# Attention followed by a squared-relu feed-forward layer, float32, one core: fewer rows and fewer waits for the first values, and other times for four half sums

## The chip, the cores and the metric

The kernel runs on one core of one Trainium2 chip. The metric is the time of one execution on the device in microseconds; several executions are timed and their median is given. One further execution is taken by the hardware profiler, and all profile lines come from it.

A core has engines that run side by side, each with its own queue of instructions in a fixed order: PE (matrix products, with PEld for its weight loads), DVE, ACT and POOL (elementwise work), and SP, which here issues all transfers. The transfers are carried out by 16 DMA engines. An instruction waits at the head of its queue until its operands are there, and everything behind it waits with it.

## The reference

```
# q, k, v: (4, 8, 768, 64), w_in: (512, 2048), w_out: (2048, 512), all float32
k_sum = k.reshape(B, H, 24, 32, D).max(axis=3)      # block maxima of the keys
v_sum = v.reshape(B, H, 24, 32, D).mean(axis=3)     # block means of the values
scores_l = scale * q @ k^T, only where |i - j| < 16
scores_s = scale * q @ k_sum^T + log(32)
a = softmax over [scores_l, scores_s]
x = a @ [v, v_sum]                                  # (3072 tokens, 512)
out = relu(x @ w_in) ** 2 @ w_out
```

## The kernel before

**Attention.** The 4 x 768 queries are cut into 48 groups of 64. A group's local keys are 94 rows of its batch, to which 24 block maxima are added; its values are a tile of 128 partitions with 24 rows of block means and the local values. Groups 0 to 7 are worked singly: their values lie in lent tiles, block means in rows 0 to 23 and local values from row 24 on. Later groups are worked in pairs and share three fixed value tiles in turn (`kinds["v"]`): rows 0 to 7 zero, block means in rows 8 to 31, local values from row 32 on.

**The first groups' values.** For the first 11 groups the host lays out `vF`, 128 rows for each, zeros included, and `load_v` (L648) loads all 128 rows into the tile. The block means of batch 0 come from six loads of v, products with an averaging matrix on PE (L590) and a copy by DVE (L607, task VS0). Then each group's tile gets its 24 rows of means: by a transfer on SP (`load_s`, L659) or, for groups 0, 1, 6 and 7 (`COPIED`), by a copy on POOL (`copy_s`, L662). Because `load_v` writes all rows, both wait for it as well as for the means. The scores of a group are L694 (single groups) or L721 (pairs), the product with the values is L986, and its result is split into two float32r parts, xh (L1070) and xl (L1073).

**Feed-forward.** Weights are float64-wide words that are turned into pairs of float32r tiles (loads L1116, then L1119 to L1136). The 3072 tokens are six units of 512. Units 0 and 1 are worked plainly (L1183, L1207). Units 2 and 3, and 4 and 5, are worked with Strassen-like block products that need sums of weight blocks: for the second product in L1795, and for units 4 and 5 also for the first product (L1632, the block products). The sums of w_in for the latter are made by `combine_in(p)`, one for each of eight pairs p of weight tiles: for pairs 0 to 3 from the tiles that are still in place, for pairs 4 to 7 from tiles kept in DRAM and read back (tasks IL, L1358). IR (L1362, DVE) adds the two parts of a tile, IA (L1387, DVE) makes four sums, IH (L1394, ACT) and IW (L1397, DVE) split them, IS (L1400, SP) stores them to `scr_t`. The block products load them from there in chunks (L1619). All tiles of `combine_in` come from a ring of three buffers ("t") that other steps use too.

**The order of the work.** Each step is a task with an engine, an estimated cost, a key, tasks it comes after, and buffers it takes and uses. `Plan.order` simulates the engines with these estimates: a free engine takes the ready task with the lowest key whose `begin` time has come; a transfer counts its issue, its bytes at 350 GB/s behind the earlier ones, 1.9 us of latency and `late`, an extra that a task can state (`LATE` is 5.0). The order in which tasks start in this simulation is the order in which they are emitted on each engine's queue. So a changed cost, key or dependency can change the order of later work on every engine. `IN_AT` gives the nominal time of each pair's half sums, from which the keys of its tasks are made; nominal times are not the times of the profile. The tasks named in `FIRST` (the loads LV0 to LV7 of the first values among them) go first in a written order; all other transfers begin at 16 us of the simulation at the earliest.

Of the kernel before, what the change touches and what calls it, by code (L numbers as in the profile page):

```python
# [20 lines left out]
P = 128  # L21
BLOCK = 32
WINDOW = 16
TQ = 64
LOC = TQ + 2 * WINDOW - 2
NEG = -1.0e30
LINE = 256
SQ = 32
# [4 lines left out]
EARLY = 8  # L33
FIRST_S = 10
SINGLE = 3
NV = 3
# [3 lines left out]
LATE = 5.0  # L40
# [6 lines left out]
TURNED, DEEP_TURNS = 2, 8  # L47
SOON_KEY, LATE_KEY = 2.0, 14.0
ONE_PAIRS = 13, 15, 17, 19, 21
IN_AT = 228.0, 240.0, 252.0, 334.0, 346.0, 360.0, 424.0, 438.0  # L50
EARLY_SUM = 25.0
VISITS = (
    (4, 5, 0), (5, 6, 1), (None, 7, 0), (6, 8, 0), (7, 9, 0), (8, 10, 0), (9, 11, 0), (10, 12, 0), (None, 13, 0),
# [17 lines left out]
def first_key(w, S):  # L71
    return min(max(TQ * w - WINDOW + 1, 0), S - LOC)

# [52 lines left out]
class Plan:  # L126
# [13 lines left out]
    def add(self, name, engine, cost, emit, key, after=(), take=(), use=(), size=0, begin=0.0, behind=None, late=0.0):  # L140
        t = Task(name, engine, cost, emit, key, [a for a in after if a is not None], list(take), list(use), size, begin)
        t.behind, t.late = behind, late
        t.index = len(self.tasks)
        self.tasks.append(t)
        for b in t.take + t.use:
            b.users.append(t)
        return t
# [71 lines left out]
def attention_then_relu2_ffn(  # L219
# [9 lines left out]
    nc = tc.nc  # L229
    B, DMODEL, S = kT.shape  # L230
    D = qW.shape[1] // 2
    H = DMODEL // D
    NT, DM = out.shape
    NF = wW.shape[1]
    NPAIR = H // 2
    NB = S // BLOCK
    KEYS = NB + LOC
    HALF_W = SQ + 2 * WINDOW
# [18 lines left out]
    add = plan.add  # L257

    kinds = {}
# [95 lines left out]
    for i, (v, n, _) in enumerate(VISITS):  # L355
        k = 0
# [95 lines left out]
        nc.gpsimd.memset(ends[:, FRONT + NPAIR * (NB + S) :], 0.0)  # L452

    t_ends = add("ends", "POOL", 0.3, clear_ends, -85)

# [31 lines left out]

    def clear_a():  # L490
        nc.gpsimd.memset(kinds["a"].tiles[0][:SQ, : 2 * H * SQ], 0.0)

    def clear_turns():
        x = kinds["a"].tiles[0][:SQ, : 2 * H * SQ].rearrange("c (i e) -> c i e", i=2)
# [37 lines left out]
    vs_bufs = {}  # L532
# [105 lines left out]
    def loads_v(g):  # L638

        b, w = divmod(g, NW)  # L640
        due = wanted(g)
        vv = v_bufs[g]
        early = g < EARLY

        def load_v():
            if g < vF.shape[0]:

                nc.sync.dma_start(out=vv.tile, in_=vF[g])  # L648
                return

            k0 = TQ * w - WINDOW + 1
            r0, r1 = max(0, -k0), min(P - SQ, S - k0)
            cuts = (r0, SQ, P - SQ) if r0 else (0, P - SQ) if r1 == P - SQ else (0, 2 * SQ, r1)
            for r0, r1 in zip(cuts, cuts[1:]):
                nc.sync.dma_start(out=vv.tile[SQ + r0 : SQ + r1, :], in_=vS[b, k0 + r0 : k0 + r1, :])  # L655

        def load_s():
            r = 0 if early else PAD
            nc.sync.dma_start(out=vv.tile[r : r + NB, :], in_=vs_bufs[b].tile[:NB])  # L659

        def copy_s():
            nc.gpsimd.tensor_copy(out=vv.tile[:NB, :], in_=vs_bufs[b].tile[:NB])  # L662

        lv = t_LV[g] = [
            add(f"LV{g}", "SP", 0.45, load_v, due - 20, behind=t_QL[g] if early else t_LV[g - 1][0], take=[] if early else [vv],
                use=[vv] if early else [], size=4 * (P if g < vF.shape[0] else LOC) * DM, begin=due - 36)
        ]
        if not (g < EARLY or w < NV or (b == 0 and g < EARLY + NV)):
            return
        ts = t_VS[b]  # L670
        if g not in COPIED:
            key = FIRST_LS + g if early else due - 19
            lv.append(add(f"LS{g}", "SP", 0.45, load_s, key, ts + lv, use=[vv, vs_bufs[b]], size=4 * NB * DM))
        else:
            lv.append(add(f"LS{g}", "POOL", 0.62, copy_s, due - 8, ts + lv, use=[vv, vs_bufs[b]]))

    def mask_of(g):
        w = g % NW
# [313 lines left out]
    def visit(both, then=(), block_sums=None, due=None):  # L992
# [29 lines left out]
        for x in both:  # L1022
            if x not in t_LV:
                loads_v(x)
# [239 lines left out]
    t_WC, t_WI, t_RC, t_claim = {}, {}, [], []  # L1264
# [82 lines left out]
    def combine_in(p):  # L1347

        due = IN_AT[p]
        pair = [buf("t", 3, (P, 2 * DM), F32, f"ci{p}_{k}") for k in range(2)]  # L1350
        kept = 2 * p >= NQ
        raw = []
        for k in range(2):
            f = 2 * p + k
            x, ws = pair[k], w_parts[0, f]

            def load(f=f, x=x):
                nc.sync.dma_start(out=x.tile, in_=scr_i[f])  # L1358

            def whole(x=x, ws=ws):  # L1360
                a, b = (x.tile[:, :DM], x.tile[:, DM:]) if kept else (w.tile.bitcast(F32) for w in ws)
                nc.vector.tensor_tensor(out=x.tile[:, :DM], in0=a, in1=b, op=ALU.add)  # L1362

            t = None
            behind = raw[0] if k else t_claim[-1]
            if kept:
                t = add(f"IL{p}_{k}", "SP", 0.45, load, due - 8 + 0.1 * k, [t_WI[f]], take=[x], size=8 * P * DM, begin=due - 14, behind=behind)
                t_claim.append(t)
                raw.append(t)
            t = add(  # L1370
                f"IR{p}_{k}", "DVE", 0.6, whole, due + 0.1 * k, [t, *t_W[0, f]], take=[] if kept else [x],
                use=[x] if kept else ws, behind=None if kept else behind, begin=due - 6,
            )
            if not kept:
                t_claim.append(t)
                raw.append(t)
            t_IN[p, k] = t

        def of(i, k):
            return pair[i].tile[:, k * HALF : (k + 1) * HALF]  # L1380

        def add_up():
            for to, a, b, op in (
                (of(1, 2), of(1, 0), of(1, 1), ALU.add), (of(0, 2), of(1, 2), of(0, 0), ALU.subtract),
                (of(0, 3), of(0, 0), of(1, 0), ALU.subtract), (of(1, 3), of(0, 1), of(0, 2), ALU.subtract),
            ):
                nc.vector.tensor_tensor(out=to, in0=a, in1=b, op=op)  # L1387

        t2 = add(f"IA{p}", "DVE", 1.25, add_up, due + 1, [t_IN[p, 0], t_IN[p, 1]], use=pair)
        ts = []  # L1390
        for k in range(2):

            def high(x=pair[k]):
                nc.scalar.copy(out=x.tile[:, :DM].bitcast(F32R), in_=x.tile[:, DM:])  # L1394

            def low(x=pair[k]):
                nc.vector.tensor_tensor(out=x.tile[:, DM:].bitcast(F32R), in0=x.tile[:, DM:], in1=x.tile[:, :DM], op=ALU.subtract)  # L1397

            def store(k=k, x=pair[k]):
                nc.sync.dma_start(  # L1400
                    out=scr_t[p][2 * k : 2 * k + 2].rearrange("c p w x -> p w c x"),
                    in_=x.tile.rearrange("p (w c x) -> p w c x", w=2, c=2),
                )

            t3 = add(f"IH{p}_{k}", "ACT", 0.52, high, due + 2 + 0.1 * k, [t2], use=[pair[k]])
            t4 = add(f"IW{p}_{k}", "DVE", 0.6, low, due + 3 + 0.1 * k, [t3], use=[pair[k]])
            ts.append(add(f"IS{p}_{k}", "SP", 0.45, store, due + 4 + 0.1 * k, [t4], use=[pair[k]], size=8 * P * DM))
        t_IN[p] = ts
# [582 lines left out]
```

## Time and profile before

| | |
|---|---|
| runs | 594.16, 594.57, 597.3 us, median 594.57 us |
| profiled execution | 594.56 us |
| its span, first to last instruction | 592.8 us |
| instructions | 12694 |
| PE busy | 575.0 us, 97% of the span |
| DVE, ACT, POOL busy | 411.2, 354.8, 61.5 us |
| moved by DMA | 158.63 MB, 268 GB/s |
| mean granted PE clock | 0.997 |

How to read the lines: a timeline line has start and length in us, the engine, the line of the program, the operation, what it writes and reads, the shape and the number of instructions put together; in brackets the idle time of the engine before it and what released it. SPq is SP's queue; a DMA line there is the issue of a transfer, not its course. A line of waits has the engine and line that waited, the one it waited for, and us in total, number of waits and the longest. Where a wait is for several things, the profile names the one that came last by its records, which can be another than the true one. A line of a window has its bounds and length, then busy us and number of instructions of PE, PEld, DVE, ACT and POOL, the granted PE clock, the share of time that the DMA engines were busy, and GB/s.

### The profile page before, as it was taken

The page shows a single profiled execution, that of the slowest core. Times are in us where ns is not written, and L with a number is a line of the kernel's source. Part 1 is how long each engine was busy: PE and PEld are TensorE (multiplying, and loading weights), DVE is VectorE, ACT ScalarE, POOL GpSimd, SP SyncE. Part 2 cuts the span into 40 slices and gives each one's busy share as a digit, 9 for nine tenths or more (in the row PEclk, how much of TensorE's full clock was granted, in tenths as well). Part 3 has the DMA queues.
Part 4 walks back from the last instruction along what each step waited for, and adds up shares of the span by engine and source line. Part 5 has one row for each costly group of instructions (what it writes and reads, how often), then busy time and mean ns, then how long its engine had stood idle before and what let it go on. Part 6 is the DMA issues. An engine that isn't in the chain of part 4 may idle for free.

```text
span 592.8 us, 12694 instructions
## 1 busy us (share of the span) xinstructions
PE 575.0 (97%) x4724; PEld 469.0 (79%) x4724; DVE 411.2 (69%) x652; ACT 354.8 (60%) x801; POOL 61.5 (10%) x101
## 2 busy tenths in 40 slices
PE   7879999999999999999999998999998999999996
PEld 6677888888888788888788887878887888788885
DVE  5879997864466482387775798999936523897653
ACT  1879876965454545475652665655546757755542
POOL 4400001032634720000000000000000000000000
PEclk9989999999999999999999999999999999999999
DMA  8998994779999769578998789998799865567772
GB/s 310 324 350 270 328 310 160 234 210 369 329 355 318 260 202 326 190 250 274 329 310 239 245 288 329 351 345 265 233 342 338 275 194 159 150 195 228 197 224 99
DMA packets 98667, 158.63 MB, mean 268 GB/s; under 512 B 9791, under 2 KB 54591, under 8 KB 98606
## 3 DMA queue, kind: packets, MB, share of 16 engines
q1 hardware_dynamic: 98606, 157.82, 82.0%
q8 instruction: 38, 0.62, 0.4%
q14 instruction: 23, 0.19, 0.1%
HBM read 112.16 MB, written 45.88 MB: 267 GB/s over the span
## 4 chain that ended last, share of the span: by engine, by line
PE 85%; DMA 6%; DVE 4%; ACT 2%; SPq 1%; issue 1%; DVEq 0%
PE o L1795 25%; PE o L1207 15%; PE h L1183 14%; PE h L1481 10%; PE o L1632 10%; PE att L721 3%; PE x L986 3%; DMA ci<-scr_i 2%; DMA kb<-kT 2%; PE vps L590 1%; DMA w<-scr_s 1%; DVE kb L521 1%; PE att L986 1%; PE o L694 1%; SPq L655 1%
## 5 line engine op out<-in xcount | busy, mean ns | idle before, releaser
L1795 PE MATMUL o<-gh,w 128*128 128x512 f32 x448 | 120.9, 391 | 0.6 <-DMA w<-scr_s 0.6
L1779 ACT CAST gh<-g 128x512 fp32r<-128x512 f32 x112 | 69.0, 621 | 55.3 <-PE o L1795 34.0
L1795 PEld LDWEIGHTS o<-gh,w 128*128 128x128 f32 x448 | 83.5, 188 | 18.7 <-issue 1.1
L1784 DVE TENSOR_TENSOR gl<-g,gh 128x512 fp32r<-128x512 f32 x112 | 75.3, 685 | 20.1 <-ACT gh L1779 19.9
L1183 PE MATMUL h<-xh,w 128*128 128x512 f32 x240 | 74.8, 393 | 0.0
L1481 PE MATMUL h<-xh,w 128*128 128x512 f32 x224 | 69.9, 394 | 1.7 <-ACT r L1491 1.7
L1795 PE MATMUL o<-gl,w 128*128 128x512 f32 x224 | 69.2, 390 | 0.0
L1207 PE MATMUL o<-w,gh 128*128 128x512 f32 x240 | 61.8, 393 | 0.0
L908 ACT ACTIVATE p<-p,nm 128x88 f32<-128x88 f32 x120 | 42.7, 357 | 18.1 <-DVE nm L902 18.1
L1183 PEld LDWEIGHTS h<-xh,w 128*128 128x128 f32 x240 | 44.6, 188 | 10.0 <-DVE w L1136 0.2
L1207 PEld LDWEIGHTS o<-w,gh 128*128 128x128 f32 x240 | 44.5, 188 | 9.9 <-DVE w L1136 0.3
L1481 PEld LDWEIGHTS h<-xh,w 128*128 128x128 f32 x224 | 41.6, 188 | 10.9 <-ACT r L1491 1.9
L1795 PEld LDWEIGHTS o<-gl,w 128*128 128x128 f32 x224 | 42.0, 188 | 9.0 <-DVE gl L1784 0.2
L1183 PE MATMUL h<-xl,w 128*128 128x512 f32 x120 | 46.7, 389 | 0.0
L1491 ACT ACTIVATE r<-h 128x512 f32<-128x512 f32 x32 | 19.1, 596 | 41.1 <-PE h L1481 41.1
L1481 PE MATMUL h<-xl,w 128*128 128x512 f32 x112 | 43.6, 389 | 0.0
L1632 PE MATMUL o<-w,w 128*128 128x512 f32 x140 | 34.8, 391 | 0.0
L1207 PE MATMUL o<-w,gl 128*128 128x512 f32 x120 | 33.5, 389 | 0.0
L1197 DVE TENSOR_TENSOR gl<-r,gh 128x512 fp32r<-128x512 f32 x30 | 23.5, 787 | 14.2 <-ACT gh L1194 9.3
L1772 DVE TENSOR_TENSOR g<-g 128x512 f32<-128x512 f32 x48 | 32.2, 685 | 0.8
L1274 POOL TENSOR_TENSOR cr<-w 128x512 f32<-128x512 f32 x16 | 23.3, 1475 | 80.0 <-DVE w L1136 72.2
L1632 PEld LDWEIGHTS o<-w,w 128*128 128x128 f32 x140 | 26.1, 188 | 6.3 <-DVE u L1664 0.5
(195 smaller groups left out, 982.4 us busy)
## 6 DMA issues: line engine op xcount, KB each, us to landing
raw<-wW SPq DMA_DIRECT2D x32, 512.0 KB
w<-scr_s SPq DMA_DIRECT2D x64, 256.0 KB
w<-scr_a SPq DMA_DIRECT2D x48, 256.0 KB
w<-scr_i SPq DMA_DIRECT2D x38, 256.0 KB
scr_t<-ci SPq DMA_DIRECT2D x16, 512.0 KB
turn<-ta SPq DMA_DIRECT2D x80, 96.0 KB
a<-turn SPq DMA_DIRECT2D x20, 384.0 KB
w<-scr_t SPq DMA_DIRECT2D x28, 256.0 KB
```

Source lines behind the costliest of these rows:

```text
L908: nc.scalar.activation(x, x, AF.Exp, bias=nm.tile[:, n : n + 1], accum_out=nm.tile[:, H + n : H + n + 1])
L986: nc.tensor.matmul(x_of(i)[h % 2 * D : (h % 2 + 1) * D, h // 2, :], lhsT=v_bufs[g].tile[:rows, h * D : (h + 1) * D], rhs=av[:rows, 2 * c : ...
L1183: nc.tensor.matmul(cut(h), lhsT=lhs.tile[:, k * P : (k + 1) * P], rhs=rhs[:, k, c0 : c0 + n], start=(i == 0), stop=(i == 3 * KT - 1),)
L1197: lambda: nc.vector.tensor_tensor(out=cut(gl), in0=cut(r), in1=cut(gh).bitcast(F32), op=ALU.subtract),
L1207: nc.tensor.matmul(o_of(o, t), lhsT=terms[i][0].tile[:, (t - t0) * P : (t - t0 + 1) * P], rhs=terms[i][1].tile, start=(first and i == 0), ...
L1274: nc.gpsimd.tensor_tensor(out=raw.tile[:, k * DM : (k + 1) * DM], in0=ws[k][0].tile.bitcast(F32), in1=ws[k][1].tile.bitcast(F32), op=ALU.add)
L1481: nc.tensor.matmul(h.tile, lhsT=lhs.tile[:, k * P : (k + 1) * P], rhs=rhs[:, k, c0 : c0 + TU], start=(i == 0), stop=(i == 3 * KT - 1),)
L1632: nc.tensor.matmul(o.tile[:, bank], lhsT=chunk.tile[:, w * HALF + d * P : w * HALF + (d + 1) * P], rhs=xs[y][d], start=starts and i == 0, ...
L1772: lambda x=x, ins=ins, op=op: nc.vector.tensor_tensor(out=x.tile, in0=ins[0].tile, in1=ins[1].tile, op=op),
L1779: f"GH{s}_{n}", "ACT", 0.54, lambda x=x, gh=gh: nc.scalar.copy(out=gh.tile, in_=x.tile), due - 4, ready,
L1784: lambda x=x, gh=gh, gl=gl: nc.vector.tensor_tensor(out=gl.tile, in0=x.tile, in1=gh.tile.bitcast(F32), op=ALU.subtract),
L1795: nc.tensor.matmul(o.tile[:, d], lhsT=chunk.tile[:, w * HALF + d * P : w * HALF + (d + 1) * P], rhs=y.tile, start=begins and w == 0 and y ...
```

## The change

Three things change.

1. `vF` holds 96 rows (`FULL`) for each of the first 11 groups instead of 128, and `load_v` writes only these rows (from row 24 on for groups 0 to 7, from row 32 on for groups 8 to 10). The zero rows that the later groups need come from a new task "pads" on POOL, which clears 32 rows of the three fixed value tiles once. The tasks that put block means into a tile wait for the means (and the pads), not for the tile's values. For groups from 8 on the transfer of means is kept behind the issue of the values' load; the POOL copies of groups 6 and 7 get a `begin` of 20.5. The estimated bytes of every value load become those of 96 rows.
2. The nominal times of the half sums of w_in change: pairs 3, 4 and 5 from 334, 346 and 360 to 330, 344 and 358, pairs 6 and 7 from 424 and 438 to 444 and 456.
3. The loads of pairs 4 to 7 get a key 16 us ahead of the nominal time instead of 8, a `begin` 20 us ahead instead of 14, and count as landing 5 us later.

```diff
+FULL = 96
...
-IN_AT = 228.0, 240.0, 252.0, 334.0, 346.0, 360.0, 424.0, 438.0
+IN_AT = 228.0, 240.0, 252.0, 330.0, 344.0, 358.0, 444.0, 456.0
...
+    t_pads = []
...
+    def clear_pads():
+        for x in kinds["v"].tiles:
+            nc.gpsimd.memset(x[:SQ], 0.0)
+
+    t_pads.append(add("pads", "POOL", 0.8, clear_pads, -70))
...
-                nc.sync.dma_start(out=vv.tile, in_=vF[g])
+                r = NB if early else SQ
+                nc.sync.dma_start(out=vv.tile[r : r + FULL], in_=vF[g])
...
-                use=[vv] if early else [], size=4 * (P if g < vF.shape[0] else LOC) * DM, begin=due - 36)
+                use=[vv] if early else [], size=4 * FULL * DM, begin=due - 36)
...
-            lv.append(add(f"LS{g}", "SP", 0.45, load_s, key, ts + lv, use=[vv, vs_bufs[b]], size=4 * NB * DM))
+            lv.append(add(
+                f"LS{g}", "SP", 0.45, load_s, key, ts + t_pads, use=[vv, vs_bufs[b]], size=4 * NB * DM,
+                behind=None if early else lv[0],
+            ))
         else:
-            lv.append(add(f"LS{g}", "POOL", 0.62, copy_s, due - 8, ts + lv, use=[vv, vs_bufs[b]]))
+            lv.append(add(
+                f"LS{g}", "POOL", 0.62, copy_s, due - 8, ts, use=[vv, vs_bufs[b]], begin=20.5 if g > 1 else 0.0
+            ))
...
-                t = add(f"IL{p}_{k}", "SP", 0.45, load, due - 8 + 0.1 * k, [t_WI[f]], take=[x], size=8 * P * DM, begin=due - 14, behind=behind)
+                t = add(f"IL{p}_{k}", "SP", 0.45, load, due - 16 + 0.1 * k, [t_WI[f]], take=[x], size=8 * P * DM, begin=due - 20, behind=behind, late=LATE)
...
-    vF = np.zeros((EARLY + NV, P, H * D), v.dtype)
+    vF = np.zeros((EARLY + NV, FULL, H * D), v.dtype)
```

More of the change, by code (lines that the diff above doesn't have):

```diff
@@ L1962 @@
             k0 = first_key(g, S)
-            vF[g, S // BLOCK : S // BLOCK + LOC] = vS[0, k0 : k0 + LOC]
+            vF[g, :LOC] = vS[0, k0 : k0 + LOC]
         else:
             k0 = TQ * g - WINDOW + 1
-            vF[g, SQ:] = vS[0, k0 : k0 + P - SQ]
+            vF[g] = vS[0, k0 : k0 + FULL]
     w_in, w_out = inputs["moe_w_in"], inputs["moe_w_out"]
```

## The prediction

> **What bounds the kernel now.** I read the page first, then the waits of PE, then the busy time by stages, and last the order of time around each wait that the change can touch.
>
> ```profile
> PE 575.0 (97%) x4724; PEld 469.0 (79%) x4724; DVE 411.2 (69%) x652; ACT 354.8 (60%) x801; POOL 61.5 (10%) x101
> PE att L986 <- ACT t L1119: 2.6, 1, 2.6
> PE h L1481 <- ACT r L1491: 1.7, 1, 1.7
> PE o L1632 <- DVE v L1664: 1.7, 1, 1.7
> PE att L986 <- DVE nm L784: 1.5, 1, 1.5
> ```
>
> PE is busy for 575.0 of 592.8 us and the change takes no matmul away, so all that it can win lies in PE's 17.8 us of idle time. The waits show where: four single waits of 2.6, 1.7, 1.7 and 1.5 us. The stages say when:
>
> ```profile
> 10.00:20.00 10.00, 9.36 (x188) 6.08 (x188) 8.26 (x23) 5.67 (x27) 4.22 (x13) 1.00 1.04 365
> 20.00:30.00 10.00, 7.99 (x224) 6.71 (x224) 8.48 (x27) 8.39 (x37) 2.76 (x4) 1.00 0.97 318
> 30.00:40.00 10.00, 6.51 (x96) 5.90 (x85) 6.97 (x15) 7.36 (x21) 0.00 (x0) 0.83 1.00 388
> 40.00:60.00 20.00, 20.00 (x107) 16.89 (x105) 19.30 (x31) 19.54 (x47) 0.00 (x0) 1.00 0.86 268
> 360.00:380.00 20.00, 18.25 (x108) 14.72 (x107) 17.98 (x33) 13.44 (x35) 0.00 (x0) 1.00 1.02 330
> 380.00:400.00 20.00, 19.40 (x138) 15.47 (x137) 19.02 (x33) 11.10 (x18) 0.00 (x0) 1.00 1.05 357
> 440.00:460.00 20.00, 18.30 (x81) 14.82 (x80) 11.35 (x20) 13.00 (x24) 0.00 (x0) 1.00 0.98 350
> ```
>
> The columns are PE, PEld, DVE, ACT, POOL, the granted clock, the DMA share and GB/s. From 10 to 40 us the DMA engines are full (1.04, 0.97, 1.00) and PE idles 6.1 of 30 us; from 40 us on PE has no idle at all, so what the start wins moves everything behind it. The other two waits stand at 360 to 380 and 440 to 460 us, again with full DMA engines. The change works on all three places.
>
> **Part 1, the first groups' values.** The eight early loads (L648) and three later ones shrink from 128 to 96 rows of 2 KB, the block means (L659, L662) no longer wait for them.
>
> ```profile
> qvpa_lent<-vF SPq DMA_DIRECT2D x8, 256.0 KB
> 16.24 0.81 DVE L607 COPY fv_lent<-vps 24x256 f32<-24x256 f32 x2
> 18.01 1.74 SPq L659 DMA_DIRECT2D qvpa_lent<-fv_lent  x2
> 22.53 2.15 SPq L659 DMA_DIRECT2D qvpa_lent<-fv_lent  x2
> 25.52 0.81 SPq L1116 DMA_DIRECT2D raw<-wW  x2
> SPq L1116 <- DMA qvpa_lent<-fv_lent: 0.3, 1, 0.3
> 23.75 0.38 PE L694 MATMUL o<-first 64*64 64x118 f32 x8
> 23.93 0.41 DVE L1073 TENSOR_TENSOR xl<-att,xh 128x256 fp32r<-128x256 f32 x1
> 25.64 1.23 PE L986 MATMUL att<-qvpa_lent 118*64 118x64 f32 x32 [1.51 <-DVE nm L784]
> ```
>
> The wait of 1.5 us is the value product of group 2 at 25.64. The profile names DVE, but the weight load that SP issues at 25.52 had itself waited for a copy of block means, the transfer issued eight before it (SP takes its eight semaphores in turn, so a transfer waits for the eighth before it to land). That copy, issued at 18.01, so landed at about 25.5, after 7.5 us in the queue, and it is this that PE waited for. The means were ready at 17.05 (16.24 + 0.81) and SP took them up at 18.01, so the old wait for the values cost nothing here; the time went in the queue behind earlier loads. Ahead of that copy stand eight value loads, each 64 KB smaller now: 0.524 MB, at 365 GB/s 1.44 us, at 318 GB/s 1.65 us. PE was free at 24.13 and the previous group's low half, which the same instruction counts on DVE, ended at 24.34. So the gain lies between 0 (the landing hangs on something else) and 1.51; I take 25.64 - 24.34 = 1.30.
>
> Moved with it: the two copies issued at 22.53 (2.15 us of SP) can now be issued with the first two, ahead of one q load and two weight loads. That pushes these three by up to 2.15 us on SP, less what the smaller loads give back. I take nothing: their users come behind the PE wait treated next. If that cover is gone, up to 2.15 - 1.44 = 0.7 us comes back.
>
> ```profile
> 6.40 0.52 POOL L491 MEMSET a<- 32x512 f32 x1
> 22.56 0.60 POOL L662 COPY qvpa_lent<-fv_lent 24x512 f32<-24x512 f32 x1 [0.68 <-DMA qvpa_lent<-vF]
> ```
>
> The three new clears have the shape of the row at 6.40: 3 x 0.52 = 1.56 us on POOL right behind it, where POOL then waits for PE's first scores. Uncovered they would hold back the first softmax by at most that; I take 0. The two copies from 22.56 on lose up to 0.68 us of waiting each on POOL, which no one on PE waits for: 0.
>
> The next wait, 2.6 us, is the one I leave:
>
> ```profile
> 32.71 1.78 PE L986 MATMUL att<-qvpa_lent 118*64 118x64 f32 x32 [2.55 <-ACT t L1119]
> q8 instruction: 1, 0.02, 1.9%
> 29.58:32.99 3.41, 0.86 (x49) 0.62 (x37) 3.31 (x11) 2.76 (x11) 0.00 (x0) 1.00 0.90 333
> 32.99:36.41 3.42, 3.42 (x40) 3.30 (x36) 1.18 (x3) 1.79 (x5) 0.00 (x0) 0.50 1.04 420
> ```
>
> The copies of means for groups 4 and 5 were issued from 22.53 on and, at 7.5 us like the first, had landed by 31; ACT's L1119 has no part in this product. The row of queue q8 is that of the stretch 29 to 33 us: one piece of PE's instruction stream comes in there, through the same full DMA engines. I read the 2.55 us as PE waiting for its instructions: it starts when PE has used up what it holds, and moves with PE. It keeps its length, so the 1.30 us pass through it. Behind it the clock is granted at half for 3.42 us; that costs up to 1.71 us of PE and I leave it too.
>
> **Part 2, half sums of pairs 3 to 5** (nominal 334, 346, 360 to 330, 344, 358; for the pairs read back from DRAM the load is planned 16 instead of 8 us ahead and counted as landing 5 us later).
>
> ```profile
> 355.48 0.40 SPq L1358 DMA_DIRECT2D ci<-scr_i  x1
> 361.82 0.69 DVE L1362 TENSOR_TENSOR ci<-ci 128x512 f32<-128x512 f32 x1 [1.82 <-DMA ci<-scr_i]
> 366.91 0.88 DVE L902 TENSOR_REDUCE nm<-p 128x8 f32<-128x704 f32 x1
> 368.89 0.57 ACT L1491 ACTIVATE r<-h 128x512 f32<-128x512 f32 x1
> 369.52 0.74 PE L1481 MATMUL h<-xh,w 128*128 128x512 f32 x2 [1.75 <-ACT r L1491]
> ```
>
> DVE stands still for 1.82 us in front of pair 4's second sum, whose load was issued at 355.48 and took 6.3 us. All behind it on DVE is late by that: the row maximum at 366.91, then the exponentials on ACT, then the relu queued behind them at 368.89, which frees the bank that PE wants: 1.75 us. The planner counted 0.45 + 1.50 + 1.90 = 3.85 us for this load (the program's constants); with 5 more it counts 8.85, over the 6.3 measured, so the sum moves behind its landing in DVE's order. Gain 1.75 at most. At the other end a sum that waits as now (1.82) in 380 to 400, where DVE has 0.98 us free, costs 0.84. I take 1.75: the one wait has one cause and the edit is larger than it.
>
> **Part 3, pairs 6 and 7** (424, 438 to 444, 456, loads as in part 2).
>
> ```profile
> 435.70 0.88 SPq L1358 DMA_DIRECT2D ci<-scr_i  x1
> 440.94 0.69 DVE L1362 TENSOR_TENSOR ci<-ci 128x512 f32<-128x512 f32 x1 [1.45 <-DMA ci<-scr_i]
> 444.22 0.69 DVE L1362 TENSOR_TENSOR ci<-ci 128x512 f32<-128x512 f32 x1 [2.59 <-DMA ci<-scr_i]
> 447.80 0.68 DVE L1664 TENSOR_TENSOR v<-o,v 128x512 f32<-128x512 f32 x1
> 464.88 0.71 SPq L1400 DMA_DIRECT2D scr_t<-ci  x1
> 483.19 4.40 SPq L1619 DMA_DIRECT2D w<-scr_t  x4
> ```
>
> The same picture: DVE waits 1.45 and 2.59 us for loads (435.70 to 444.22 is 8.5 us), and the sum at 447.80, which frees PE's bank, is late by enough to cost PE 1.70 us. Counted as 8.85 us and sought 20 us later, these sums no longer stand in front of their loads. DVE is busy 11.35 of 20 us here, so the work itself finds room. What is late next: the last store, issued at 464.88, comes up to 18 us later, 482.9, and the loads that first need it are issued from 483.19 on, ahead of PE's use. Bounds: 1.70 gained, or 0 when the loads are issued later too and DVE meets them as now. I take 1.70.
>
> **The sum.** 1.30 + 1.75 + 1.70 = 4.75 us. The profiled execution took 594.56 us (span 592.8 and 1.76 around it), the median of the runs is 594.57: 594.56 - 4.75 = 589.8 us.
>
> **Rivals.** (a) The start gives nothing: the freed queue is filled by weight loads of 512 KB, which keep eight in flight, and PE's next instructions come as late as before, so the second wait swallows the first's gain. For it: a larger load ahead costs 0.524 MB/333 GB/s = 1.57 us, as much as the gain. Against it: the stream of instructions is also asked for earlier. Time: 594.56 - 3.45 = 591.1.
>
> (b) More goes than I take: the shifted idle time no longer falls into one stretch of the clock, and the half-rate stretch after it is gone: 589.8 - 1.71 = 588.1. For it: PE was busy 0.86 of 3.41 us ahead of the half rate, and 1.30 us earlier it would be 2.2. Against it: where the stretches begin may differ between executions. [...] And if the 2.55 us are not the instruction stream but a landing behind the values, they go too: 589.8 - 2.55 - 1.71 = 585.5. [...]
>
> (c) One of the two DVE waits stays or turns up elsewhere, since every order after the start is worked out anew: 594.56 - 1.30 - 1.70 = 591.6, with a new wait of 1 us 592.6.
>
> (d) Slower: the last batch's keys.
>
> ```profile
> 282.70 3.52 SPq L958 DMA_DIRECT2D turn<-ta  x4
> 289.35 0.90 PE L721 MATMUL att<-kb,q 64*32 64x128 f32 x44 [0.52 <-DVE kb L521]
> ```
>
> PE already waits 0.52 us at 289.35 for keys, so their loads have no slack; the planner sets them by costs that change. Put behind the turned store that now follows them (282.70, 3.52 us) and the two loads of 512 KB that go with such a step (3.1 us at 333 GB/s), PE would wait 6.6 us more: 594.56 - 4.75 + 6.6 = 596.4. From a slip of 4.75 us it decides. Against it: nothing in the edit names these loads.
>
> **How the numbers follow.** Forecast 0.42, (a) 0.16, (b) 0.11, (c) 0.19, (d) or another wait of its size 0.12. About 0.5%, 3.0 us, is what a measurement of this kernel can tell from no change. Faster by more than that: the forecast, (b), and most of (a), whose 591.1 is just beyond: 0.62. Within: (c) and the rest of (a): 0.25. Slower: the upper part of (d) and of (c): 0.13. The range leaves out (d), the worst of (c), and 585.5: 587.8 to 594.0; for the forecast alone 588.8 to 590.8.
>
> **What would show it.** Right: PE's value product of groups 2 and 3 starts within 0.3 us of PE being free, near 24.3; the wait of about 2.5 us with a q8 row in it still follows, near 29 to 31; no DVE wait for ci<-scr_i above 0.5 us; PE's waits on L1491 and L1664 gone; the last scr_t store before 483. Wrong: a value product that still waits over 1 us near 25.5, new PE waits in 40 to 280 us, where there are none now, a DVE wait for ci<-scr_i again, or a wait for keys near 289 that has grown.

## The result, and the profile after

The change made the kernel slower: 598.58 us (median of 20 runs, 594.60 to 603.29) against 594.37 us for the kernel before in the same session (20 runs, 591.30 to 597.97). The ratio is 1.0068, with a 95% interval of 1.0045 to 1.0090. The ratios in this document are worked out from the single runs and leave out the few slow executions (at most one of a kernel, two of before beside it), so they are not quotients of the medians. The profiled execution of after took 598.27 us, its span 596.5. The forecast was 589.8 us, faster. Lines of the program that are named here stand 9 to 14 lower in after: L648 is now L657, L659 L668, L1119 L1133, L986 L1000, L1358 L1372, L1664 L1678, L1795 L1809; in the kernels with a written order further down they are another 33 lines lower, and in rows96_only up to 3 lower than in before.

The page's busy times:

```profile
PE 576.2 (97%) x4724; PEld 468.9 (79%) x4724; DVE 409.3 (69%) x652; ACT 354.9 (59%) x801; POOL 63.2 (11%) x104
```

The waits of PE (what waited and for what; us in all, times, the longest):

```profile
PE x L1000 <- DMA a<-turn: 2.3, 1, 2.3
PE att L1000 <- DMA raw<-wW: 2.1, 1, 2.1
PE x L1000 <- DMA w<-scr_s: 1.5, 1, 1.5
PE o L1809 <- DMA w<-scr_s: 1.5, 2, 0.9
PE t L863 <- DVE qvpa_lent L852: 1.3, 1, 1.3
PE o L1646 <- DVE u L1678: 0.9, 1, 0.9
```

The wait for ACT's relu (1.7) is gone, as forecast, that of the value product of group 2 (1.5) has given way to one of 0.8 for ACT, and the one near 450 us has fallen from 1.7 to 0.9. New ones stand in their place: transposes at the start that wait for DVE, and attention products in the second half that wait for transfers. By stages (PE, PEld, DVE, ACT, POOL, granted clock, DMA share, GB/s):

```profile
10.00:20.00 10.00, 9.36 (x188) 6.08 (x188) 8.26 (x23) 5.74 (x26) 4.42 (x14) 1.00 1.06 297
20.00:30.00 10.00, 7.13 (x148) 6.21 (x152) 7.08 (x21) 7.49 (x34) 1.76 (x4) 0.83 0.93 281
30.00:40.00 10.00, 7.10 (x167) 6.20 (x160) 7.38 (x20) 6.96 (x20) 0.00 (x0) 1.00 1.02 366
360.00:380.00 20.00, 19.89 (x114) 15.81 (x112) 18.47 (x34) 14.42 (x38) 0.00 (x0) 1.00 1.02 320
380.00:400.00 20.00, 17.02 (x127) 13.65 (x127) 16.70 (x30) 9.70 (x17) 0.00 (x0) 1.00 1.03 331
400.00:420.00 20.00, 17.73 (x132) 14.37 (x131) 17.70 (x29) 10.83 (x18) 0.00 (x0) 1.00 0.91 264
440.00:460.00 20.00, 19.08 (x84) 15.33 (x83) 10.37 (x18) 13.55 (x24) 0.00 (x0) 1.00 0.90 321
```

Two rows are to be read against those of before. From 10 to 20 us the DMA engines are as full as they were (1.06 against 1.04), but move 297 instead of 365 GB/s: the fewer bytes take the same time. This row parts all the profiles below in the same way: 295 to 322 GB/s in the ten kernels that load 96 rows, 353 to 395 in the eight that load 128. From 380 to 420 us PE is idle for 5.25 us where it was idle for 0.6, with DMA engines at 1.03 and 0.91, while 360 to 380 has gained 1.64. The row of before from 400 to 420 us:

```profile
400.00:420.00 20.00, 20.00 (x142) 16.26 (x142) 19.63 (x33) 11.87 (x20) 0.00 (x0) 1.00 0.87 261
```

The start of after in its timeline:

```profile
19.32 3.27 SPq L668 DMA_DIRECT2D qvpa_lent<-fv_lent  x4
22.73 0.43 DVE L1136 TENSOR_SCALAR raw<-raw 128x512 uint32<-128x512 uint32 x1 [2.01 <-DMA raw<-wW]
22.73 0.69 ACT L1133 ACTIVATE t<-raw 128x512 f32<-128x512 f32 x1 [2.51 <-DMA raw<-wW]
23.07 0.65 DVE L852 TENSOR_TENSOR qvpa_lent<-qvpa_lent,nm 128x472 f32<-128x472 f32 x1
23.48 1.24 SPq L1130 DMA_DIRECT2D raw<-wW  x2
23.86 0.63 PE L863 MATMUL t<-first,qvpa_lent 128*128 128x128 f32 x4 [1.30 <-DVE qvpa_lent L852]
26.77 1.98 PE L1000 MATMUL att<-qvpa_lent 118*64 118x64 f32 x32 [0.85 <-ACT qvpa_lent L833]
34.57 1.15 PE L1000 MATMUL att<-qvpa_lent 118*64 118x64 f32 x32 [2.13 <-DMA raw<-wW]
```

DVE and ACT stand still for 2.0 and 2.5 us in front of the first weight tile. Behind it on DVE is the multiplication that ends a group's softmax (L852), and PE's transposes wait 1.30 us for that. The four copies of block means now stand in one row at 19.32, and the second weight load follows at 23.48. In the timeline of before the same conversion stood further back in both queues and did not wait, and the second weight load was issued 3.1 us earlier:

```profile
20.36 1.41 SPq L1116 DMA_DIRECT2D raw<-wW  x2
22.05 0.68 ACT L1119 ACTIVATE t<-raw 128x512 f32<-128x512 f32 x1
22.71 0.75 DVE L1122 TENSOR_SCALAR raw<-raw 128x512 uint32<-128x512 uint32 x1
```

The large part of the loss in this one profile, 380 to 420 us, is not where the loss of the median lies, as the experiments show.

### The profile page after: what moved, and what is told of

It reads as the page before. It is cut to its first block, busy times and chain, and to the rows that moved or that the text cites. A ratio compares the mean times of both kernels' runs of the same rounds, so it can differ in the third digit from the quotient of the medians.

```text
span 596.5 us, 12696 instructions
## 1 busy us (share of the span) xinstructions
PE 576.2 (97%) x4724; PEld 468.9 (79%) x4724; DVE 409.3 (69%) x652; ACT 354.9 (59%) x801; POOL 63.2 (11%) x104
## 4 chain that ended last, share of the span: by engine, by line
PE 80%; DMA 13%; DVE 4%; SPq 1%; ACT 1%; issue 1%; DVEq 0%
PE o L1809 22%; PE o L1221 15%; PE h L1197 14%; PE o L1646 11%; PE h L1495 10%; DMA w<-scr_s 3%; PE att L735 3%; PE x L1000 3%; DMA kb<-kT 2%; DMA raw<-wW 1%; DMA a<-turn 1%; DMA q<-qW 1%; DMA qvpa_lent<-vF 1%; DMA scr_t<-ci 1%; DMA ci<-scr_i 1%; DMA fv_lent<-vS 1%
## 5 line engine op out<-in xcount | busy, mean ns | idle before, releaser
L1809 PE MATMUL o<-gh,w 128*128 128x512 f32 x448 | 121.0, 391 | 1.6 <-DMA w<-scr_s 1.5
L1809 PEld LDWEIGHTS o<-gh,w 128*128 128x128 f32 x448 | 83.3, 188 | 20.3 <-ACT gh L1793 2.1
L1809 PE MATMUL o<-gl,w 128*128 128x512 f32 x224 | 69.2, 389 | 0.0
L1809 PEld LDWEIGHTS o<-gl,w 128*128 128x128 f32 x224 | 42.0, 188 | 8.8
L1646 PE MATMUL o<-w,w 128*128 128x512 f32 x140 | 34.5, 390 | 0.0
L1211 DVE TENSOR_TENSOR gl<-r,gh 128x512 fp32r<-128x512 f32 x30 | 22.3, 743 | 14.8 <-ACT gh L1208 11.8
```

Of the source, the lines that this page charges most:

```text
L1211: lambda: nc.vector.tensor_tensor(out=cut(gl), in0=cut(r), in1=cut(gh).bitcast(F32), op=ALU.subtract),
L1646: nc.tensor.matmul(o.tile[:, bank], lhsT=chunk.tile[:, w * HALF + d * P : w * HALF + (d + 1) * P], rhs=xs[y][d], start=starts and i == 0, ...
L1809: nc.tensor.matmul(o.tile[:, d], lhsT=chunk.tile[:, w * HALF + d * P : w * HALF + (d + 1) * P], rhs=y.tile, start=begins and w == 0 and y ...
```

## The experiments

Single executions of one and the same kernel spread by up to 10 us, so times come from 6 to 12 runs each, beside 23 to 35 runs of the kernel before in the same job. The two kernels of loads alone have one run each.

**First four: is it the shape of the loads, part 1, or the half sums?** Theory 1: 96 rows are no faster. Theory 2: the half sums run into full transfers.

```diff
# rows_alone: eight loads of `rows` rows to row `first`, then the next shape
+    nc.sync.dma_start(out=x[first : first + rows, g * DM : (g + 1) * DM], in_=vF[g, :rows])
# rows96_only: before, and
-    nc.sync.dma_start(out=vv.tile, in_=vF[g])
+    nc.sync.dma_start(out=vv.tile[NB : NB + 96], in_=vF[g, NB : NB + 96])     # g < 8
# first_values_only: after, with IN_AT and the loads IL of before
# half_sums_only: before, with IN_AT and the loads IL of after
```

rows_alone:

> The loads alone, nothing of the attention computed: eight loads of rows of 2 KB in a row, then the next shape when they have landed. Theory 1 (96 rows are no faster than 128, since the rows do not spread evenly over what the transfers run through): eight loads of 128 rows at 402 GB/s take 2.10 MB / 402 = 5.2 us plus a latency, eight of 96 rows from row 24 just as long or longer (1.57 MB at 240 GB/s: 6.6 us). Rival (a load costs its bytes, the low rate came from the other loads around): 1.57 MB / 402 = 3.9 us, 1.3 us less than 128 rows. [...]

rows96_only:

> The kernel before, with the loads of the first eight groups' values cut to the 96 rows from row 24; the order of all work, and who waits for whom, is that of before. Theory 1: the transfer rate from 10 to 20 us falls from 365 to about 300 GB/s, the value product of group 2 starts no earlier than 25.6, and the time is 594.4 to 596. Rival (the other order of the transfers, not the shape, lowered the rate): the rate stays near 365, the queue is 1.3 us ahead by 25 us, and the time is 593.1.

first_values_only:

> Part 1 of the change alone (96 rows, clears, block means that do not wait), the half sums as before. By the lags of the trace after (+0.8 us from 115 to 290 us, before the half sums come in) theory 1 gives 595.2, at most 596.5. Rival (the start is worth the 1.30 us that was forecast and the loss comes from elsewhere): 593.1.

half_sums_only:

> Parts 2 and 3 alone (other times for the half sums of pairs 3 to 7), the first values as before; the order up to some 344 us is that of before. Theory 2 (once DVE no longer waits, PE waits for transfers in the second products, because the moved loads and stores push other transfers back): the DVE wait of 1.8 us is gone, PE waits some 3 us more between 375 and 420 us, the end gains 0.8, and the time is about 596.5. Rival (these waits arise only in the order and lag that part 1 makes): 594.4 - 1.75 - 0.8 = 591.8.

The timeline of rows_alone; each DVE copy ends a stretch of eight loads (second pass: 128 rows from 84.46 to 93.29, then 96 from row 24, 96 from row 32, 96 from row 0, 64 from row 32, 64 from row 64):

```profile
84.29 0.17 DVE L25 COPY y<-x 128x8 f32<-128x8 f32 x1 [5.61 <-DMA x<-vF]
93.29 0.17 DVE L25 COPY y<-x 128x8 f32<-128x8 f32 x1 [8.82 <-DMA x<-vF]
101.91 0.17 DVE L25 COPY y<-x 128x8 f32<-128x8 f32 x1 [8.45 <-DMA x<-vF]
110.71 0.17 DVE L25 COPY y<-x 128x8 f32<-128x8 f32 x1 [8.62 <-DMA x<-vF]
119.37 0.17 DVE L25 COPY y<-x 128x8 f32<-128x8 f32 x1 [8.49 <-DMA x<-vF]
126.87 0.17 DVE L25 COPY y<-x 128x8 f32<-128x8 f32 x1 [7.33 <-DMA x<-vF]
134.49 0.17 DVE L25 COPY y<-x 128x8 f32<-128x8 f32 x1 [7.44 <-DMA x<-vF]
```

Eight loads of 96 rows take 8.45 us, of 128 rows 8.82: 0.37 us less, where a price by bytes asks for 1.3. (The first pass, not shown, gives 7.71 against 8.21.) Much of these times is not bytes, since eight loads of 16 rows took 5.1 and 5.7 us in the same run; so this kernel does not show what 96 rows cost in a full queue. Where the rows lie made no difference in this run (8.45, 8.62 and 8.49 for 96 rows from row 24, 32 and 0; 7.33 and 7.44 for 64 rows from row 32 and 64). So 96 rows alone are hardly faster than 128, as theory 1 has it, but the uneven spread of the rows that it gives as the reason is not shown: that was the author's conjecture.

In the kernel, rows96_only took 594.86 us, ratio 0.9998 (0.9972 to 1.0024): no loss of the size of after's, and no gain that can be told, though one of 1.3 us (0.9978) lies just inside the interval. Its rate from 10 to 20 us falls nearly as in after, and the first weight comes as late (stages, then timeline):

```profile
10.00:20.00 10.00, 9.44 (x192) 6.18 (x196) 8.23 (x24) 6.18 (x28) 4.24 (x13) 1.00 1.07 311
```

```profile
23.70 0.68 ACT L1122 ACTIVATE t<-raw 128x512 f32<-128x512 f32 x1 [2.12 <-DMA raw<-wW]
23.70 0.43 DVE L1125 TENSOR_SCALAR raw<-raw 128x512 uint32<-128x512 uint32 x1 [1.06 <-DMA raw<-wW]
25.19 1.23 PE L989 MATMUL att<-qvpa_lent 118*64 118x64 f32 x32 [1.66 <-ACT qvpa_lent L859]
```

In the order of before, ACT waits 2.12 us for it and DVE 1.06, and the value product of group 2 waits 1.66 us for a copy by ACT that stands behind the conversion. In before the same product waited 1.51 us (at 25.64), so one wait has taken the place of another, and PE has lost little by it. So no gain of the shape can be measured, and alone no loss. first_values_only: 599.83 us, 1.0082 (1.0050 to 1.0114): the whole loss is in part 1. half_sums_only: 595.01 us, 1.0011 (0.9983 to 1.0040): theory 2 falls as a cause of the loss, and the 3.45 us forecast for these two parts did not come either.

**Next four: the order of the work.** Theory 3: part 1 loses by the new order, not by its loads or clears. The planner derives a new order from part 1. Its orders with and without part 1 hold the same tasks up to 250 us of its own time, so they can be put together there. These kernels emit a written list of tasks. Up to 250 the lists differ thus: SP takes up the means LS4, LS5, LS8, LS9 and LS10 earlier; ACT converts the first weight (WM0_0, L1119 in before) ahead of XH0 and WH0_0 ahead of XH2, DVE converts WR0_0 (L1122) ahead of XL0 and N3, WR0_1 and WW0_0 ahead of XL2; single places on other tasks follow. From 250 on: LS36 to LS38 earlier, and ten places around 355 to 365.

```diff
# Plan.order, in all four; SEQ is the written list
-        return started
+        return [named[n] for n in SEQ]
# order_of_before:      part 1, list of before, "pads" added
# new_order_to_250:     part 1, new list to 250, list of before behind it
# new_order_from_250:   part 1, list of before to 250, new list behind it
# after_with_old_start: after,  list of before to 250, its own behind it
```

order_of_before:

> Part 1 as in first_values_only (96 rows, clears, means that wait for no values), but every engine works in the order of the kernel before, written out; only the clears are added. Theory 3 (part 1 loses by the order that the planner derives from it, not by the loads or clears): 594.4 to 595.6, as rows96_only. Rival (the clears on POOL hold back the first softmax, or the means land where others need the queue): near 599.

new_order_to_250:

> Part 1 with the planner's new order for the work planned up to 250 us and the order of before for the rest. If theory 3 holds and the start is where it loses (block means issued in one row at 19 to 22 us, weights converted ahead of the first groups' results): 598 to 599.5. If the loss lies in the end of the order: 594.4 to 595.6.

new_order_from_250:

> Part 1 with the order of before for the work planned up to 250 us and the planner's new order for the rest, which differs there in three copies of block means taken up 3 us earlier (LS36 to LS38) and in some ten places on DVE and ACT around 355 to 365. If the loss lies at the end: 598 to 599.5, with PE waits between 365 and 420 us; if at the start: 594.4 to 595.6.

after_with_old_start:

> The kernel after, all three parts, with the order of before for the work planned up to 250 us. If the loss lies at the start: 594 to 595 (half_sums_only was 595.0). If it lies at the end: 598, as after.

| kernel | median us (runs) | ratio to before (95%) |
|---|---|---|
| order_of_before | 596.64 (12) | 1.0016 (0.9990 to 1.0043) |
| new_order_to_250 | 600.79 (12) | 1.0067 (1.0035 to 1.0099) |
| new_order_from_250 | 594.77 (12) | 0.9995 (0.9972 to 1.0017) |
| after_with_old_start | 595.24 (12) | 0.9991 (0.9968 to 1.0014) |

This settles the place: the same loads, clears and dependencies cost nothing that can be measured in the old order, and the new order costs its 4 us in its first 250 us alone. The end of after's order, where its profile shows the most idle time, loses nothing over many runs: after_with_old_start has just that end.

**Next four: which part of the new order?** Theory 4: the conversions on DVE and ACT that were put ahead of their weight.

```diff
# bytes_in_plan_only: before, and in the task LV
-    size=4 * (P if g < vF.shape[0] else LOC) * DM
+    size=4 * 96 * DM
# new_conversions_only:  order_of_before, DVE and ACT in the new order to 32
# after_old_conversions: after, DVE and ACT in the order of before to 32
# after_counted_128: after, and in the task LV
-    size=4 * FULL * DM
+    size=4 * (P if g < vF.shape[0] else LOC) * DM
```

bytes_in_plan_only:

> The kernel before, with one number changed: the bytes that the planner counts for a values' load are those of 96 rows. No transfer, no tile and no dependency differs; 128 rows are loaded. Theory 4 (the planner now expects the first weight load 0.524 MB / 350 GB/s = 1.5 us sooner than it lands, and puts its conversion, WM0_0 on ACT and WR0_0 on DVE, in front of the softmax of groups 3 and 4, which then wait 2 to 3 us for the transfer): 598 to 599.5, with the wait for raw<-wW at 20 to 23 us on DVE and ACT. Rival (it is the early copies of block means on SP that cost the time, LS8 to LS10 above all, which stay here): 594.4 to 595.6.

new_conversions_only:

> Part 1 with the written order of before (as order_of_before), but DVE and ACT in the new order for what is planned up to 32 us: WR0_0 and WM0_0 ahead of XL0 and XH0, WH0_0 ahead of XH2, WW0_0 and WR0_1 earlier. SP and PE work in the order of before. Theory 4: 598 to 600. Rival (SP's order): 594.4 to 596.6.

after_old_conversions:

> The kernel after in its own order, but DVE and ACT in the order of before for what is planned up to 32 us (the opposite swap). SP keeps the new order, with the block means in one row. Theory 4: the wait for raw<-wW in front of the softmax is gone and the time is 594 to 595, or less, if the earlier block means are worth the 1.30 us of the forecast: 593. Rival: 598, as after.

after_counted_128:

> The kernel after with one number put back: the planner counts the values' loads as 128 rows again, while 96 are loaded. The planner then puts the first conversions where before had them; but it orders much of PE's, DVE's and ACT's later work anew as well. Theory 4: 594 to 595.5, with no wait for raw<-wW ahead of the softmax of groups 3 and 4. Rival: 598.

| kernel | median us (runs) | ratio to before (95%) |
|---|---|---|
| bytes_in_plan_only | 596.67 (12) | 1.0020 (0.9990 to 1.0050) |
| new_conversions_only | 598.49 (6) | 1.0079 (1.0049 to 1.0110) |
| after_old_conversions | 597.20 (12) | 1.0056 (1.0031 to 1.0081) |
| after_counted_128 | 601.63 (6) | 1.0124 (1.0088 to 1.0160) |

The swap of a few conversions is enough to lose it all (new_conversions_only), by the wait that theory 4 names:

```profile
23.34 0.68 ACT L1166 ACTIVATE t<-raw 128x512 f32<-128x512 f32 x1 [3.31 <-DMA raw<-wW]
24.47 1.09 PE L896 MATMUL t<-first,qvpa_lent 128*128 128x128 f32 x4 [2.11 <-DVE qvpa_lent L885]
```

But theory 4 falls as the only cause, twice. Undoing the swap in after gave back nothing sure (1.0056), so what this kernel keeps costs too: SP's new order, and that of every engine after 32 us (parts 2 and 3 it keeps as well). And the planner's count alone, which makes the same swap, cost 1.0020 (0.9990 to 1.0050) where 598 us and more was expected. Its row shows the difference: with 128 rows loaded, the weight is there 2.7 us earlier.

```profile
20.65 0.70 ACT L1119 ACTIVATE t<-raw 128x512 f32<-128x512 f32 x1 [1.06 <-DMA raw<-wW]
```

after_counted_128 was a miss of its own: with the old count the planner orders much of PE's, DVE's and ACT's work up to 250 anew, with the means in a row on SP, and PE waited 3.0 us for the value product at 26.60. It is a third order, not the old one.

**Next four: the new orders with 128 rows.** Theory 5: the new order loses where it meets the lateness that 96 rows bring.

```diff
# after_rows128, new_conversions_rows128, after_old_conversions_rows128:
# the kernel of that name, and (vF of 128 rows laid out as in before)
-    r = NB if early else SQ
-    nc.sync.dma_start(out=vv.tile[r : r + FULL], in_=vF[g])
+    r = 0 if early else SQ
+    nc.sync.dma_start(out=vv.tile[r:], in_=vF[g, r:])
# rows_mixed: as rows_alone, with three loads of 128 rows of 4 KB among the eight
```

after_rows128:

> The kernel after in its own order on every engine, but the first eight groups' values are loaded as 128 rows again (zeros included), so that their block means wait for them by the data. Theory 5 (loads of 96 rows let the first weight load land some 2 us later, at 22.3 to 24.0 instead of 20.6 to 21.4, and the loss comes where the new order meets that lateness): the first weight lands at 20.6 to 21.5, DVE and ACT wait under 1.1 us for it, and the time is 594 to 596. Rival (the new order loses by itself): 598.

new_conversions_rows128:

> new_conversions_only (part 1, order of before on SP and PE, the new order of conversions on DVE and ACT up to 32 us), with 128 rows loaded. Theory 5: 594.5 to 596, against 598.5 with 96 rows. Rival (the new order of conversions loses by itself): 598.5.

after_old_conversions_rows128:

> after_old_conversions (SP in the new order, conversions in the old), with 128 rows loaded. Theory 5: 594 to 595.5. Rival (four copies of block means in a row, each 0.8 to 1.0 us of SP, put the second and third weight load 2 us back, and that costs the same whatever the rows): 597 to 598.

rows_mixed:

> Loads alone, nothing of the attention computed: eight loads of rows of 2 KB with three of 128 rows of 4 KB among them, as at the start of the kernel, for 128 rows, 96 from row 24, 96 from row 32 and 112 from row 16, each three times. If 96 rows slow the larger loads behind them: the stretch with 96 rows takes longer than that with 128. If only the bytes count: (2.10 + 1.57) / (1.57 + 1.57), 14% less than with 128 rows. By the loads alone (0.83 against 0.87 us each): 0.3 us less.

The timeline of rows_mixed; each copy ends a stretch of eleven loads (128 rows from 52.30, 96 from row 24, 96 from row 32, 112 from row 16, 128 again, 96 from row 24):

```profile
52.30 0.17 DVE L28 COPY y<-x 128x8 f32<-128x8 f32 x1 [13.51 <-DMA x<-vF]
65.32 0.17 DVE L28 COPY y<-x 128x8 f32<-128x8 f32 x1 [11.82 <-DMA x<-vF]
78.82 0.17 DVE L28 COPY y<-x 128x8 f32<-128x8 f32 x1 [12.13 <-DMA w<-wF]
92.67 0.17 DVE L28 COPY y<-x 128x8 f32<-128x8 f32 x1 [12.65 <-DMA w<-wF]
108.18 0.17 DVE L28 COPY y<-x 128x8 f32<-128x8 f32 x1 [14.37 <-DMA w<-wF]
119.84 0.17 DVE L28 COPY y<-x 128x8 f32<-128x8 f32 x1 [10.49 <-DMA w<-wF]
133.66 0.17 DVE L28 COPY y<-x 128x8 f32<-128x8 f32 x1 [12.54 <-DMA w<-wF]
```

From copy to copy: 128 rows 13.0 and 11.7 us, 96 rows from row 24 13.5 and 13.8, from row 32 13.9, 112 rows 15.5. Ahead of these lines and behind them, 96 rows from row 32 took 13.8 and 13.5 us, 112 rows 14.8 and 14.4. Among larger loads the smaller shapes were not only no cheaper, they took longer; this is one execution, in which the two stretches of 128 rows differ by 1.4 us. In the kernels the first weight, where an engine waits for it, is there at 20.65, 21.29 and 21.38 us with 128 rows (bytes_in_plan_only, after_rows128, new_conversions_rows128) and at 22.3 to 24.0 in every kernel with 96. A part of this is a later issue: SP issued it at 15.3 to 16.0 us in those three and at 15.5 to 17.2 in the ten with 96 rows, and from issue to use it took 5.0 to 6.1 us against 5.8 to 7.5.

| | 128 rows | 96 rows |
|---|---|---|
| old order | 1 (before) | 0.9998, 1.0016 |
| new conversions, old SP | 1.0056 (1.0027 to 1.0085) | 1.0079 |
| old conversions, new SP | 1.0029 (0.9998 to 1.0061) | 1.0056 |
| both new (after) | 1.0049 (1.0016 to 1.0081) | 1.0068 |

Each 128-row kernel of a new order in the table stands 0.2% below its twin, within the intervals, and two of them still lose; bytes_in_plan_only, a new order with 128 rows too, cannot be told from before (1.0020). Theory 5 is right on the lateness and not enough for the loss: the new order loses something by itself. The traces part 96 rows from 128 more sharply than the runs' medians, since all later noise is left out. The start of PE's 1045th matmul (by that count nearly the same work is done in each), in one profile each: in the old order to 250, 96.6 to 100.1 us (eight kernels, mean 98.7; before 100.1); in a new order with 96 rows, 100.6 to 103.8 (six, mean 102.3; after 100.6); in a new order with 128 rows, 96.9 to 100.6 (four, mean 99.1). By 100 us the 96-row kernels of a new order are 3.6 us behind, as much as the medians say. Those with 128 rows are 0.4 us behind, so these traces do not show where their 0.2 to 0.6% go.

Not all of the 3.6 us is waiting. In these profiles the granted clock is at half in stretches of 3.41 or 6.83 us. In the first 100 us of the old order five kernels of eight have one of 3.41 us, the others none; the six of a new order with 96 rows have 3.41 to 10.24 us each, four of them two or three times before's. In after it is this one, behind the wait of 1.30 us:

```profile
26.56:29.97 3.41, 3.20 (x60) 3.11 (x64) 3.16 (x9) 3.41 (x18) 0.00 (x0) 0.50 0.98 312
```

The means are 6.26 us at half clock against 2.13; at 0.50 the difference is worth up to 2.1 of the 3.6 us, an estimate from these stretches. Over the runs the share is smaller. The time lost to the clock, (1 - granted clock) x span, is on average 5.0 us in new_order_to_250 against 3.3 in before beside it, 5.1 against 2.8 in new_conversions_only, but 3.3 in after, where before has 2.8 to 3.4 in the other jobs.

**Last two: the half sums, each part alone.**

```diff
# last_pairs_only: before, with 444 and 456 in IN_AT and the new loads IL for p >= 6
# pairs_3_to_5_only: before, with 330, 344 and 358 and the new loads IL for p < 6
```

last_pairs_only:

> Part 3 alone: the later half sums and earlier loads for pairs 6 and 7, everything else as before. By the forecast 1.70 us less: 593.6 against 595.3. By the profiles with the new times so far (PE's wait near 450 is 0.92 us in each of them, against 1.4 to 2.2 without) 0.5 to 1.3 less: 594.0 to 594.8, inside what the runs can tell.

pairs_3_to_5_only:

> Part 2 alone: pairs 3 to 5, everything else as before. By the forecast 1.75 us less: 593.6 against 595.3. Rival (PE's wait for ACT's relu near 370 goes, 2.06 us in most runs of the old times, but PE then waits as long for transfers, a<-turn and w<-scr_s, between 365 and 417 us, where the DMA engines are full): 595.3, no difference, with PE waits on a<-turn or w<-scr_s of 1.5 us and more in its profile.

last_pairs_only took 595.67 us, 1.0010 (0.9981 to 1.0039); pairs_3_to_5_only 596.79, 1.0039 (1.0016 to 1.0063): no gain from either, and from pairs 3 to 5 a small loss. The attention product that follows PE's old wait tells where that gain went, first in before, then in half_sums_only, in pairs_3_to_5_only and in after:

```profile
372.36 0.89 SPq L965 DMA_DIRECT2D a<-turn  x2
380.75 1.15 PE L986 MATMUL x<-a,v 128*64 128x64 f32 x32
```

```profile
370.53 0.92 SPq L965 DMA_DIRECT2D a<-turn  x2
380.68 1.25 PE L986 MATMUL x<-a,v 128*64 128x64 f32 x32 [2.77 <-DMA a<-turn]
```

```profile
381.43 1.15 PE L986 MATMUL x<-a,v 128*64 128x64 f32 x32 [2.93 <-DMA a<-turn]
```

```profile
372.74 1.20 SPq L979 DMA_DIRECT2D a<-turn  x2
381.70 1.15 PE L1000 MATMUL x<-a,v 128*64 128x64 f32 x32 [1.53 <-DMA w<-scr_s]
416.89 1.15 PE L1000 MATMUL x<-a,v 128*64 128x64 f32 x32 [2.27 <-DMA a<-turn]
```

The product starts at 380.7 to 381.7 in all four. Its operand is fetched at 370 to 373 and takes 8 to 10 us through full DMA engines. In before PE came there 1.75 us late and found it landed; without that wait PE stands in front of it. (In after the row names another transfer at 381.70.) Behind the new wait the clock is at half for 3.41 us in half_sums_only (from 381.60) and in pairs_3_to_5_only (from 382.50), as it is behind the old wait in four other profiles; before and after have no such stretch there.

For the last pairs the wait near 450 is shorter by the edit alone:

```profile
452.58 1.19 PE L1632 MATMUL o<-w 128*128 128x512 f32 x4 [0.92 <-DVE u L1664]
```

It is 0.92 or 0.93 us in all eight profiles with the new times, and 1.06 to 2.23 in the ten with the old ones: 0.7 us less on average, less than the runs can tell. One sum still stands in front of its load, the last of pair 7 (in after; 1.5 to 3.1 us in all eight):

```profile
466.36 0.69 DVE L1376 TENSOR_TENSOR ci<-ci 128x512 f32<-128x512 f32 x1 [2.42 <-DMA ci<-scr_i]
```

PE does not wait behind it in after.

## Why the prediction was wrong, point by point

- **Part 1's term, 1.30 us: the failed step.** It priced 64 KB less for each of eight loads by the rate of the stretch (0.524 MB at 365 GB/s, 1.44 us). The rate belonged to the 128-row shape (365 GB/s from 10 to 20 us in before, 297 in after). Alone the eight loads save 0.37 us, among larger ones they lose 0.5 to 2.2 in the one run of rows_mixed, and the first weight lands later. That a transfer waits for the eighth before it to land, by which the term placed the landing of the means at 25.5, holds in the trace of before: SP waited 0.6 us ahead of the weight load at 21.44 for the one issued at 15.89, 0.7 ahead of the copy at 22.53 for the value load of 16.59, and 0.3 ahead of 25.52 for the copy of 18.01, each the eighth before. The means no longer hold up the value product of group 2 in after, but it waits 0.85 us for ACT and starts at 26.77, 1.1 us later than in before: PE had lost 1.30 us two steps earlier.
- **"Moved with it ... I take nothing": the step that set the sign.** Only three transfers on SP were followed, with 0.7 us at most to lose. That the planner, told of fewer bytes, expects the first weight 1.5 us sooner and moves its conversion in front of two groups' softmax on DVE and ACT was not looked for, though the text before the prediction says that a changed cost reorders every engine. The wait that this adds is 2.0 us on DVE and 1.3 on PE in after, and with 96 rows the new order up to 250 carries the whole loss.
- **The pads at 0:** order_of_before contains them and shows no loss that can be told (1.0016, 0.9990 to 1.0043).
- **The wait of 2.55 us, left as it is:** right in after (2.13 us). It stands before the same matmul, the 469th, in all eighteen profiles, 0.25 to 3.8 us long. In seventeen of them it ends 1.4 to 1.8 us after one q8 row has ended (at 32.71 after 31.35 in before, at 34.57 after 32.85 in after), wherever that falls between 28.8 and 34.5 us; in the eighteenth the row had ended 2 us before PE came there, and the wait is 0.25 us. This speaks for the instruction stream.
- **The half rate, left as it is:** right in after in its length (3.41 us at 0.50), not in its place: it stands ahead of this wait, behind a new one. Four of the six 96-row kernels of a new order have 6.8 us of it or more.
- **Part 2, 1.75 us:** the mechanism was right. With the old times DVE waits 1.8 to 3.4 us in front of the same sum in all ten profiles (in five the row names another transfer), with the new ones in none, and PE's wait for the relu is gone. What is late next was not named: the fetch of the attention operand, which lands 11 us later than the removed wait and takes all of it.
- **Part 3, 1.70 us:** right that PE's wait shrinks, by some 0.8 us in after. The next wait, on DVE's u at the same line, stands right behind. That the sums no longer stand in front of their loads is wrong for the last of them (2.42 us at 466.36 in after), one of the signs that the prediction gave for being wrong, though it costs PE nothing there. The last store of scr_t was issued at 475.4, before 483, as asked.
- **The rivals:** (a) said that the start gives nothing, by larger loads that fill the queue; it gives less than nothing. (b) had the half-rate stretch go; it moved, and the wait of 2.55 us stayed. That idle time within one stretch brings on the half rate was the author's reading of two rows and is not shown: in the stretch ahead of the half rate PE was busy for 0.86 of 3.41 us in before and for 1.67 of 3.42 in after. (c) named "every order after the start is worked out anew", and priced it at one wait of 1 us. (d) named the keys near 289 for the slower side; their wait fell to 0.26 us there.

What stays open: why the stretches with smaller shapes take longer in rows_mixed (13.5 to 15.5 us against 11.7 and 13.0), why the half-rate stretches come in one execution and not in the next, and how the new order's loss with 128 rows, 0.2 to 0.6%, divides between the conversions and SP's four copies of means.

## What to carry to other kernels

Price a transfer by a row of its own shape, not by bytes at the stage's rate; where no row has the shape, let the low end of the gain be below zero. In a kernel whose order is planned from estimates, an estimate that the hardware does not keep can cost more than the transfer itself: list what the new order moves, engine by engine, before pricing what the edit says. Where a wait is removed in a stage with full DMA engines, find the next operand that comes by DMA, and when it lands.

## What the runs showed of the hardware that I had not expected

Fewer rows can take longer: eight loads of 112 rows among three larger ones took 14.4 to 15.5 us where eight of 128 rows took 11.7 to 13.0, in one execution. And the stretch at half the granted clock at the start is not in every execution. It stands in before and after (0.83 in a stretch of 10 us), and not in half_sums_only, whose order up to there is that of before:

```profile
20.00:30.00 10.00, 7.89 (x224) 6.44 (x216) 9.61 (x26) 9.26 (x41) 2.05 (x4) 1.00 0.92 310
30.00:40.00 10.00, 8.35 (x113) 7.94 (x114) 8.69 (x18) 8.68 (x21) 0.00 (x0) 1.00 1.04 409
```

That execution was at the 1045th matmul at 96.6 us, 3.5 ahead of before's profile. Nor is it the same from run to run of one kernel: over 135 runs of before the mean granted clock goes from 0.989 to 1.000, and the 24 runs of the lowest (0.992 and below) have a median of 597.0 us, the 48 of the highest (0.996 and above) 594.0. So one profile of a kernel can be several us from the next at the same place, and a loss read from one of them, as the 4.6 us between 380 and 420 here, has to be confirmed by an edit.
